# Reordered loads, transposes and fill in the opening batches of an attention kernel fused with a feed-forward

## The chip, the cores and the metric

The kernel runs on one core of one Trainium2 chip. The metric is the device time of one execution in microseconds; less is better. Three runs of the kernel before gave 258.54, 258.21 and 256.69 us, a median of 258.21.

## What is computed

Two steps in a row. The attention first: for each of 8 batches and 8 heads, 32 "packed" query rows `p` attend over 576 keys and values of width 64, and the 576 rows of `q` then attend over the 32 packed results. The feed-forward follows on the 4608 rows of width 512 (8 heads x 64) that come out.

```python
p_packed = sm_attn(p, k, v)                 # softmax(p k^T / 8) v      [8, 8, 32, 64]
out = sm_attn(q, p_packed, p_packed)        #                           [8, 8, 576, 64]
x = out.transpose(0, 2, 1, 3).reshape(4608, 512)
h = x @ w_in                                # w_in  [512, 2048]
g = h * cos(h)
result = g @ w_out                          # w_out [2048, 512], fp32 out
```

## The kernel before

The eight batches pass one after another through the same steps, and the kernel writes the order of every instruction by hand (there is no scheduler: each engine runs its instructions in the order in which the source emits them, and waits where an operand is missing). Matmuls are in bf16. PSUM has eight banks: two belong to the output tiles (`ot`), six are handed out either as three pairs (`psA`) or as six single banks (`psH`); `banks(3)` and `banks(0)` change between the two.

The steps of one batch `b`:

- `load(n, b)`: a DMA that GpSimd issues brings k, q or v to SBUF and casts it to bf16. The v and q buffers are single: the next load waits until the last one has been read. All such DMAs go through GpSimd's queue in order, and reuse eight semaphores in turn, so that the ninth waits for the first to land.
- `pe_T`: k and q are transposed on TensorE in three groups of eight 96x96 blocks, each group copied out of PSUM by the engine named (later batches use the transposing DMA, `xbar`). `permute_v` rearranges v, on VectorE for batch 0 and on GpSimd after that.
- `dup_p`, `pack_p`: the packed rows p are cast, doubled, transposed and kept in `P2`.
- `s1`: scores of p against k, and the exponential on ScalarE (tile `a`, its sums beside it). `a1_pe` or `a1_one` transposes these probabilities on TensorE into `a1T`; `recips` takes reciprocals of the sums; `pp` multiplies by v and copies the result into `ppT`.
- `s2`: scores of q against `ppT`, the exponential (`a2u`); `sums2` takes the sums by a matmul and their logarithm; `normalise` turns these into the reciprocal on ScalarE and writes the weights `a2n` on VectorE.
- `ppw(b, n)`: `ppT` times quarter n of `w_in`, copied to `PPW`. With it, h is `PPW` times `a2n` and never needs the attention's output itself.
- the h steps: for each of 16 slices `fc` of the 2048 columns, matmuls into PSUM, the cosine on ScalarE (`cosT`) and the product on VectorE (`gT`). Batch 0 uses `h_one` (512 of 576 columns, one `psH` bank each; the other 64 columns come later in `h_rest`), the others `h_mm`, inside `slot`.
- the output: `gT` times `w_out`, 16 matmuls of 128x512 for each 128 rows, one bank `ot`. These matmuls are the fill: `fill(n)` emits the next n of them between other work, `set_filler(b)` starts the generator of batch b, and `fill(1000)` emits all that is left. `slot` spreads what is left over its 16 h steps.

Batch 0 has no earlier batch to fill with. There `warm(n)` emits n matmuls on zeros, whose result is not used. The opening is straight-line code, lines 385 to 464, then `slot(1, ...)`, the opening of batch 2 at lines 505 to 533, and a regular loop from line 537. In the opening, `a1_one(1)` at line 436 transposes the probabilities of batch 1 into the two halves of one `psA` pair; after it come `banks(0)` and the 16 `h_one` steps, with the packed blocks `ppw(0, 1..3)` after steps 1, 5 and 9 and `pp(1)` after step 13:

```python
    a1_one(1)
    recips(1)
    banks(0)
    for fc in range(NFC):
        h_one(0, fc)
        if fc in (1, 5, 9):
            ppw(0, 1 + fc // 4, (ACT, V), own=True)
        if fc == 13:
            pp(1, own=True, engs=(ACT, ACT))
    ACT.preload_act_table_set(EXP_SET)
    pe_T("q", 1, (ACT, V, V), own=one)
```

## Time and profile before

| what | value |
|---|---|
| profiled execution, its own time | 258.04 us |
| its span | 256.3 us |
| median of three runs (range) | 258.21 us (256.69 to 258.54) |
| TensorE busy, matmuls | 235.0 us, 92% |
| VectorE busy | 161.4 us, 63% |
| ScalarE busy | 174.3 us, 68% |
| GpSimd busy | 56.3 us, 22% |
| DMA moved | 37.09 MB, mean 145 GB/s |
| q-load of batch 0 lands, first q transposes | 14.02 us |
| first `h_one` matmul of batch 0 | 24.29 us |
| `s2` of batch 1 begins | 40.19 us |
| second half of the first `h_mm` of batch 1 begins | 48.75 us |

In the views, PE is TensorE's matmuls, PEld its weight loads, DVE is VectorE, ACT ScalarE, POOL GpSimd, SP the engine that issues output DMAs. A row of a timeline is start, duration, engine, source line, operation, output tile, input tile, shapes, and how many instructions are merged; in brackets, how long the engine stood idle before it and what released it. The chain of waits is the path that ended last, followed back from the end: start, duration, what. Line 86 is the copy helper on VectorE, line 84 on ScalarE.

### The profile page before, as it was taken

Reading aid. Unit: us, or ns where it says so; the run is one execution under the profiler, and the core shown is the slowest. Engines: PE = TensorE matmul, PEld = TensorE weight load, DVE = VectorE, ACT = ScalarE, POOL = GpSimd, SP = SyncE. Lnnn points to the kernel's source line nnn. Section 1 sums busy time; section 2 is a strip of 40 time slices with the busy share of each in tenths; the row PEclk is TensorE's granted clock in tenths of the full one; section 3 lists DMA queues with packets and bytes.
Section 4 is the critical chain, followed back from the end, with each engine's and each line's share of the span. In section 5 each row is a group of like instructions: output and inputs, shape, how many; then the busy total and the mean of one; then the engine's idle time right before and its main releaser. Section 6 shows DMA issues by size and latency. Waiting matters only on the chain.

```text
span 256.3 us, 5021 instructions
## 1 busy us (share of the span) xinstructions
PE 235.0 (92%) x2000; PEld 130.0 (51%) x2035; DVE 161.4 (63%) x239; ACT 174.3 (68%) x293; POOL 56.3 (22%) x67
## 2 busy tenths in 40 slices
PE   8684876899998999999999999999999999999993
PEld 3452242366553565456545654465546554665452
DVE  3456984677656778757875667568857765675000
ACT  2366897576736888788888767788788675975110
POOL 8253611340070040504050303103310000000000
PEclk9999797999999999999999999999999999999999
DMA  7999999999679999499969993999692111202133
GB/s 102 202 206 205 205 207 224 204 151 185 135 131 202 215 169 224 96 192 166 196 141 196 167 221 77 154 199 139 141 169 71 41 43 41 75 18 62 52 84 82
DMA packets 63159, 37.09 MB, mean 145 GB/s; under 512 B 35776, under 2 KB 58560, under 8 KB 63136
## 3 DMA queue, kind: packets, MB, share of 16 engines
q0 software_dynamic: 23152, 18.75, 48.2%
q1 hardware_dynamic: 39824, 17.90, 33.5%
q8 instruction: 16, 0.26, 0.4%
q10 hardware_dynamic: 160, 0.13, 0.2%
q14 instruction: 7, 0.06, 0.1%
HBM read 37.22 MB, written 9.44 MB: 182 GB/s over the span
## 4 chain that ended last, share of the span: by engine, by line
PE 76%; DVE 9%; ACT 6%; DMA 4%; issue 3%; POOL 1%; DVEq 0%; ACTq 0%; POOLq 0%
PE ot L346 43%; PE psA L261 21%; DMA qbf<-in_q_dram 4%; DVE gT L291 2%; DVE PPW L86 2%; PE psA L141 2%; PE psA L214 2%; PE psA L240 2%; DVE gT L268 1%; PE psA L190 1%; PE ot L332 1%; DVE a2n L250 1%; ACT cosT L265 1%; PE psH L287 1%; ACT a2u L232 1%
## 5 line engine op out<-in xcount | busy, mean ns | idle before, releaser
L346 PE MATMUL ot<-w_out_bf,gT 128*128 128x512 bf16 x482 | 128.4, 383 | 2.0 <-issue 0.9
L268 DVE TENSOR_TENSOR gT<-psA,cosT 128x576 bf16<-128x576 f32 x112 | 83.3, 757 | 34.5 <-ACT cosT L265 33.5
L265 ACT ACTIVATE cosT<-psA 128x576 bf16<-128x576 f32 x112 | 72.5, 652 | 26.2 <-PE psA L261 24.6
L261 PE MATMUL psA<-a2n,PPW 128*128 128x288 bf16 x448 | 73.4, 286 | 1.2 <-DVE PPW L86 0.4
L346 PEld LDWEIGHTS <-gT 128*128 128x128 bf16 x512 | 47.9, 98 | 43.3 <-issue 7.0
L261 PEld LDWEIGHTS <-PPW 128*128 128x128 bf16 x448 | 43.7, 98 | 31.2 <-issue 2.0
L86 DVE CAST PPW<-psA 128x1024 bf16<-128x1024 f32 (+1 forms) x23 | 25.8, 1129 | 12.1 <-PE psA L214 12.0
L272 POOL COPY joint<-gT 128x512 bf16<-128x512 bf16 x14 | 8.6, 611 | 104.4 <-DVE gT L268 104.4
L86 DVE COPY osb<-ot 128x512 f32<-128x512 f32 (+1 forms) x14 | 9.4, 672 | 21.3 <-PE ot L332 17.4
L84 ACT COPY osb<-ot 128x512 f32<-128x512 f32 (+1 forms) x23 | 13.2, 574 | 13.5 <-PE ot L346 12.4
L86 POOL COPY vp<-vbf 96x3072 bf16<-96x3072 bf16 x7 | 19.3, 2750 | 3.5 <-DMA vbf<-in_v_dram 3.5
L250 DVE SCALAR_TENSOR_TENSOR a2n<-a2u,r,lns 128x576 bf16<-128x576 bf16 x16 | 12.7, 833 | 5.8 <-ACT lns L248 5.8
L242 ACT ACTIVATE lns<-psA 128x576 f32<-128x576 f32 x16 | 10.4, 650 | 7.3 <-PE psA L240 6.7
L150 ACT ACTIVATE a<-psA 128x576 bf16<-128x576 f32 x16 | 10.2, 646 | 4.2 <-PE psA L141 4.2
L84 ACT CAST ppT<-psA 64x128 bf16<-64x128 f32 x24 | 6.2, 259 | 9.2 <-DVE ppT L86 5.6
L346 PE MATMUL ot<-w_out_bf,joint 128*128 128x512 bf16 x47 | 12.4, 380 | 0.0
L232 ACT ACTIVATE a2u<-psA,rs 128x576 bf16<-128x576 f32 x16 | 11.0, 736 | 1.8 <-PE psA L214 0.8
L291 DVE TENSOR_TENSOR gT<-psH,cosT 128x512 bf16<-128x512 f32 x16 | 10.2, 685 | 2.5 <-ACT cosT L290 2.4
L290 ACT ACTIVATE cosT<-psH 128x512 bf16<-128x512 f32 x16 | 8.9, 604 | 3.8 <-PE psH L287 3.4
L287 PE MATMUL psH<-a2n,PPW 128*128 128x512 bf16 x30 | 9.2, 426 | 2.1 <-DVE PPW L86 1.2
L214 PE MATMUL psA<-w_in_bf,ppT 64*32 64x512 bf16 x224 | 10.4, 381 | 0.5 <-DVE gT L268 0.5
L248 ACT ACTIVATE lns<-lns 128x576 f32<-128x576 f32 x16 | 10.0, 674 | 0.0
(80 smaller groups left out, 178.1 us busy)
## 6 DMA issues: line engine op xcount, KB each, us to landing
kbf<-in_k_dram POOLq DMA_DIRECT2D x8, 576.0 KB, 12.3
vbf<-in_v_dram POOLq DMA_DIRECT2D x8, 576.0 KB, 8.0
qbf<-in_q_dram POOLq DMA_DIRECT2D x8, 576.0 KB, 9.8
out_dram<-osb SPq DMA_DIRECT2D x24, 192.0 KB, 2.9
out_dram<-osb SPq DMA_DIRECT2D x22, 128.0 KB, 2.4
w_in_bf<-in_moe_w_in_dram POOLq DMA_DIRECT2D x4, 512.0 KB, 16.7
w_out_bf<-in_moe_w_out_dram POOLq DMA_DIRECT2D x4, 512.0 KB, 20.7
out_dram<-osb SPq DMA_DIRECT2D x26, 64.0 KB, 2.2
```

The costliest lines, as they stand in the source:

```text
L84: ACT.copy(out=out, in_=in_)
L86: eng.tensor_copy(out=out, in_=in_)
L214: nc.tensor.matmul(ps[y][32 * x:32 * x + 32, :], ppT[b % 2][r, 2 * x + y, :], w_in_bf[r, x, n * 512:(n + 1) * 512], start=True, stop=True)
L232: ACT.activation(out=a2u[b][:, y].rearrange("p (e x) -> p e x", e=2), in_=ps[y][:, :, 0:HS], func=AF.Exp, scale=rs1[b][:, y:y + 1])
L242: ACT.activation(out=lns[b][:, y].rearrange("p (e x) -> p e x", e=2), in_=ps[:, :, 0:HS], func=AF.Ln)
L250: V.scalar_tensor_tensor(out=a2n[b][:, y], in0=a2u[b][:, y], scalar=r1[b][:, y:y + 1], in1=lns[b][:, y], op0=ALU.mult, op1=ALU.mult)
L261: nc.tensor.matmul(ps[:, e, 0:HS], PPW[b][:, y, fc * 128:(fc + 1) * 128], a2n[b][:, y, e * HS:(e + 1) * HS], start=(y == 0), stop=(y == 1))
L265: ACT.activation(out=csv, in_=ps[:, :, 0:HS], func=AF.Sin, bias=PI_HALF)
L268: V.tensor_tensor(out=gT[b][:, fc, :].rearrange("p (e x) -> p e x", e=2), in0=ps[:, :, 0:HS], in1=csv, op=ALU.mult)
L287: nc.tensor.matmul(ps, PPW[b][:, y, fc * 128:(fc + 1) * 128], a2n[b][:, y, 0:512], start=(y == 0), stop=(y == 1))
L291: V.tensor_tensor(out=gT[b][:, fc, 0:512], in0=ps, in1=cs, op=ALU.mult)
L346: nc.tensor.matmul(pss[c], w, w_out_bf[:, fc, :], start=(fc == 0), stop=(fc == NFC - 1))
```

## The change

- At the start the load of p by SP takes only batch 0's rows; batch 1's come by a separate load on GpSimd's queue after k of batch 1, and are cast by VectorE (`dup_p(2, 4, V)`) after `s2(0)` and packed (`pack_p(1, 2, ...)`) after the k transposes of batch 1, in place of one of two `warm` matmuls.
- The last quarter of `w_in` is loaded before v of batch 1, not after it.
- The probabilities of batch 1 are transposed by `a1_pe` into two single `psH` banks; `a1_one` goes.
- `ppw(0, 1..3)` come after h steps 0, 4 and 8; `pp(1)` after the last h step; q of batch 1 is copied out by VectorE alone, and the load of the exponential's table on ScalarE comes after that in the source.
- Of the fill before `slot(1, ...)` (4, 4 and 6 around `ppw(1, 1)` and `normalise(1)`), the four ahead of `ppw(1, 1)` go to the end (4 and 10).
- In batch 2's opening, `fill(6)` after `pp(2)` becomes `fill(8)`, and `fill(4)` moves from behind `recips(3)` to ahead of `s1(3)`.

```diff
-    def a1_pe(b, ys=(0, 1)):
+    def a1_pe(b, ys=(0, 1), own=None):
...
-            ps = psa(BF16)[:, 0, :]
+            ps = own(BF16) if own else psa(BF16)[:, 0, :]
...
-    def a1_one(b):
-        t = a1T[b] = att_pool.tile([128, 2, C, 128], BF16, name="a1T", tag="a1T")
-        ps = psa(BF16)
-        for y in range(2):
-            for c in range(C):
-                nc.tensor.transpose(ps[0:TP, y, c * 128:(c + 1) * 128], a1[b % 2][:, y, c, 0:TP], ident)
-            copy(V, t[0:TP, y].rearrange("p c x -> p (c x)"), ps[0:TP, y, 0:C * 128])
...
-    nc.sync.dma_start(out=p_raw[:, 0:4, :], in_=p_rows[:, 0:4, :])
+    nc.sync.dma_start(out=p_raw[:, 0:2, :], in_=p_rows[:, 0:2, :])
...
     load("k", 1)
+    G.dma_start(out=p_raw[:, 2:4, :], in_=p_rows[:, 2:4, :])
...
-    dup_p(0, 4, V)
-    pack_p(0, 2)
+    dup_p(0, 2, V)
+    pack_p(0, 1)
...
-    load("v", 1)
     load_w_in(3)
+    load("v", 1)
...
     s2(0)
+    dup_p(2, 4, V)
...
-    warm(2)
+    pack_p(1, 2, bank(BF16))
+    warm(1)
...
-    a1_one(1)
-    recips(1)
     banks(0)
+    a1_pe(1, own=one)
+    recips(1)
     for fc in range(NFC):
         h_one(0, fc)
-        if fc in (1, 5, 9):
+        if fc in (0, 4, 8):
             ppw(0, 1 + fc // 4, (ACT, V), own=True)
-        if fc == 13:
-            pp(1, own=True, engs=(ACT, ACT))
+    pp(1, own=True, engs=(ACT, ACT))
+    pe_T("q", 1, (V, V, V), own=one)
     ACT.preload_act_table_set(EXP_SET)
-    pe_T("q", 1, (ACT, V, V), own=one)
...
     sums2(1, 1)
-    fill(4)
     ppw(1, 1, V)
     fill(4)
     normalise(1)
     ACT.preload_act_table_set(SIN_SET)
-    fill(6)
+    fill(10)
...
     pp(2)
-    fill(6)
+    fill(8)
...
     normalise(2)
+    fill(4)
     s1(3)
     ACT.preload_act_table_set(SIN_SET)
     a1_xbar(3)
     recips(3)
-    fill(4)
```

More of the change, by code (lines that the diff above doesn't have):

```diff
@@ L408 @@
     permute_v(0, V)
+    load_w_in(3)
     load("v", 1)
-    load_w_in(3)
     warm(3)
@@ L435 @@
     rest_ppw()
-    a1_one(1)
+    banks(0)
+    a1_pe(1, own=one)
     recips(1)
-    banks(0)
     for fc in range(NFC):
         h_one(0, fc)
-        if fc in (1, 5, 9):
+        if fc in (0, 4, 8):
             ppw(0, 1 + fc // 4, (ACT, V), own=True)
-        if fc == 13:
-            pp(1, own=True, engs=(ACT, ACT))
+    pp(1, own=True, engs=(ACT, ACT))
+    pe_T("q", 1, (V, V, V), own=one)
     ACT.preload_act_table_set(EXP_SET)
-    pe_T("q", 1, (ACT, V, V), own=one)
     load("v", 2)
```

## The prediction

> **What bounds the kernel now.** The page first: where TensorE idles, and where its clock drops.

> ```profile
> PE   8684876899998999999999999999999999999993
> ...
> PEclk9999797999999999999999999999999999999999
> ```

> One digit is 6.4 us. From slice 8 (51 us) TensorE is at nine tenths to the end: there a microsecond is gained only by taking away a gap or a matmul. Before it come the 4, 8, 7, 6 of slices 3 to 6, with a 7 in the clock of slices 4 and 6. All but two small edits of the change lie in this opening. So next the chain of waits, 19 to 49 us:

> ```profile
> 22.64 0.47 DVE a1T L86
> 23.11 0.04 issue
> 23.15 0.51 PE psA L182 x6
> 23.66 0.02 issue
> 23.68 0.56 DVE a1T L86
> 24.25 0.04 issue
> 24.29 1.40 PE psH L287 x4
> ...
> 39.34 0.81 ACT qT L84
> 40.15 0.04 issue
> 40.19 0.44 PE psA L141 x16
> ...
> 43.59 1.71 PE ot L346 x4
> ...
> 45.72 1.23 DVE PPW L86
> ```

> Three places. At 22.64 the two halves of the probabilities go through one PSUM pair in turn: copy, transposes, copy, and only then the first h matmul (24.29). At 39.34 the scores of batch 1 wait for a q copy on ScalarE. At 43.59 four fill matmuls stand ahead of `ppw(1, 1)`, whose copy (45.72) `a2n` queues behind. The timeline of VectorE, between the first two:

> ```profile
> 31.14 2.48 DVE L291 TENSOR_TENSOR gT<-psH,cosT 128x512 bf16<-128x512 f32 x4
> 33.54 0.68 DVE L86 CAST PPW<-ot 128x512 bf16<-128x512 f32 x1
> 34.13 2.49 DVE L291 TENSOR_TENSOR gT<-psH,cosT 128x512 bf16<-128x512 f32 x4
> 37.57 1.29 DVE L291 TENSOR_TENSOR gT<-psH,cosT 128x512 bf16<-128x512 f32 x2 [0.95 <-ACT cosT L290]
> ```

> A product takes 0.60 (31.14 to 33.54 for four), a `PPW` copy 0.60. VectorE is the bound of the h steps, with 16 + 3 such pieces, 11.4 us; they took from 25.59 to 38.86, 13.27. ScalarE needs 16 x 0.56 + 3 x 0.53 = 10.6, warm TensorE 16 x 0.52 + 3 x 0.41 = 9.6.

> **The change part by part**, in times of this execution (258.04 us, 0.17 under the median).

> *Single banks.* The second half's transposes no longer wait for the first half's copy. Both halves still wait for the second exponential of `s1(1)`, 21.35 (the new tiles lie where its scores were); 12 transposes by 0.08 end at 22.5, behind VectorE's `PPW` copies (22.64). The first h matmuls follow at once, ready 0.67 later as before (24.29 to 24.96), at 23.2; ScalarE's table is in at 22.86, the cosine done at 23.8. VectorE runs two `a1T` copies (22.64 to 23.6), reciprocals (0.35), and starts products at 24.0, not 25.59: 1.6 gained.

> *Packed blocks a step sooner, `pp(1)` last.* A block's copy now has three products between it and the first step that needs it (1.8 us) where it had two (1.2), against a matmul and a cosine of 0.67 + 0.60; that should remove the short idles (0.24 and 0.16). ScalarE's four `ppT` copies (35.84, 1.08 us) move behind the last cosine and with them the 0.95 idle of VectorE. Products end at 24.0 + 11.4 + 0.3 for small gaps = 35.7, against 38.86.

> *q copies on VectorE alone.* Three copies, two of which took 1.01 together: 1.5, so `s2(1)` starts at 37.2 where it started at 40.19. ScalarE's table load (1.28) hides: `ppT` copies until 35.4, table until 36.7. **3.0 gained** up to here. The old path (table, then a 0.80 copy) would be no quicker: were the cover gone, 0.8 + 0.04 comes back.

> *Quarter before v1, p in two loads.* The queue of loads runs without a gap, about 2.9 us for a k, q or v and 2.6 for a quarter of weights: quarter 0 lands at 19.5, 1 at 22.1, 2 at 24.65, v1 at 27.5, quarter 3 at 30.2. 384 KB of p at the end took 2.7 us, so the new 64 KB cost 0.45, and everything behind moves by this. Quarter 3 then lands at 27.7, before its use at about 28.7 (after step 8); v1 at 30.5. GpSimd's copy of v1 (2.75) ends at 33.3, where it ended at 31.3; behind it in GpSimd's queue stand only loads that queue in the DMA anyway. `pp(1)` has its turn when step 15 is through, about 33.5, and must be 2.7 ahead of `s2(1)`: slack 1.2. If that cover is gone, each microsecond costs one. w_out's first chunk lands at 36.1, before the first fill at 37.8. The smaller first load frees SP nothing that the chain uses: it starts with k and q at the DMA's rate. Zero.

> *New on VectorE after `s2(0)`*: two casts, first waiting for the new p load, with the three k copies and `a2n` queued behind. It lands 0.45 after k1 (16.9): 17.35; the casts of twice the size took 0.59 for both, so 0.3; the first k copy starts at 17.65, not 17.45, and the pause before the second (0.21) takes it up. The new `P2` copy (half of a 0.42) ends at 19.7, `a2n` starts at 19.77. `s1(1)` comes 0.4 later, but ScalarE is busy until 20.20. Lowest price 0. The highest comes from line 160:

> ```profile
> 75.74 1.66 DVE L160 TENSOR_SCALAR rs<-r 128x2 f32<-128x2 f32 x1
> ```

> Its other instances take 0.17; GpSimd's copy `vp` ran from 74.61 to 77.37, when this one ended. The new casts meet GpSimd's DMA issues (0.77 each, two of them around 17.2 to 18.7); held until the end they start 1.35 late and cost 1.2. I take 0, because the casts at 3.10 ran beside GpSimd's work at 3.21 without it. [...]

> *Fill(4) behind `ppw(1, 1)`.* VectorE's copy comes up to 1.7 sooner (1.71 of fill). But the 14 fill matmuls and the block stand before the h matmuls either way, and TensorE was full from 43.59 to 47.9; the second half of the first h matmul came at 48.75. At half clock (0.43 a matmul until 45.3) they end at 48.0, not 48.75: **0.7**. At full clock the two fill matmuls between the sums take 0.43, not 0.85, which also removes ScalarE's idle of 0.68 at 43.62; the block is through at 43.3, its copy at 44.6, `a2n` 1.7 later at 46.3, and the 14 matmuls (0.216 each, 3.0) end with it: 2.4. Which one it is hangs on the clock:

> ```profile
> 21.30:24.70 3.40, 1.13 (x12) 0.76 (x11) 2.59 (x9) 1.55 (x3) 0.74 (x1) 1.00 1.27 204
> 24.70:28.20 3.50, 3.28 (x15) 0.95 (x15) 2.30 (x4) 2.46 (x5) 1.46 (x2) 0.51 1.28 209
> 38.40:41.85 3.45, 1.10 (x27) 0.65 (x29) 2.27 (x4) 2.65 (x4) 1.11 (x2) 1.00 1.24 229
> 41.85:45.30 3.45, 3.45 (x18) 1.22 (x16) 0.35 (x1) 2.77 (x5) 0.00 (x0) 0.51 1.23 219
> ```

> Columns: window, length, then busy time of PE, PEld, DVE, ACT, POOL, then clock. Twice a window with TensorE busy for a third (1.13, 1.10) is followed by one at half clock; the window from 17.9 with 2.35 was not. The first falls away (TensorE idles only 20.6 to 21.4); the second gap shrinks from 2.5 us to 1.7, so the window holds some 1.4 of work: nearer to 1.10 than to 2.35, so I take the half clock. [...]

> *Batch 2.* `fill(8)`: TensorE idled 0.35 before the scores of 78.91, which wait for ScalarE's `ppT`; two more matmuls (0.43) fill it and are taken from slot 2: 0.35. `fill(4)` ahead of `s1(3)`: its second half idled 0.38 for ScalarE's logarithm; that is filled, but the cosine of 86.13 stays where the table load puts it, and I count 0.25. From neither to both: 0 to 0.75.

> Sum: 3.0 + 0.7 + 0.35 + 0.25 = 4.3 of 258.04: **253.7 us**. Bounds: 1.2 less for the casts, 1.7 more for the clock.

> **The rivals.** (1) No half-clock window around 42 us: 258.04 - 6.0 = 252.0. For it: the gap shrinks; against: 1.4 is nearer to 1.10. (2) v1 lands behind q1 as well (33.4) and `pp(1)` becomes the bound: copy until 36.2, `s2(1)` at 38.9, 1.7 lost: 255.4. Against it: the loads land in the order of issue. (3) The h steps do not run at VectorE's pace; only the 1.6 of the banks stays: 256.4. For it: the old steps lost 1.9 to idles, ScalarE's 10.6 is close. (4) Slower: the new wait of VectorE for p. Its price is landing minus 17.55, and it is paid by k copies, `a2n` and all behind. With quarter 0 (19.95) it leaves a gain of 1.9; from 21.9 on it decides the sign; with quarter 2 (25.1) the time is 261.3. Against it: order of landing; for it: its rows are 256 bytes and were never seen between large loads.

> **How the numbers follow.** Forecast 0.40; (1) 0.27; (2) 0.12; (3) 0.11; (4) and anything slower 0.10. The range reaches from 251.5 (rival 1 without the 0.3 of gaps, batch 2's edits at their 0.75) to 257.0 (rival 3 with half the casts' 1.2); outside stays (4). This kernel's measurement tells 1%, 2.6 us, from no change. Below 255.6 lie forecast, (1) and a third of (2): 0.71; above 260.8 lies most of (4): 0.08; the rest 0.21.

> **What would show it.** First `gT` of line 283 near 24.0 and `s2` of batch 1 near 37.2; VectorE without idle between; the k copies of batch 1 still from 17.5; clock 1.0 from 24 to 28; first `h_mm` complete about 3.7 sooner than 48.75; the lead kept to the end. Wrong if VectorE idles at its `p_bf` cast, if `pp(1)` waits for `vp`, or if the lead at 50 us is lost by 100.

## The result, and the profile after

| | before | after |
|---|---|---|
| median of 20 runs each (range), us | 258.19 (255.71 to 258.86) | 256.80 (252.81 to 259.05) |
| ratio, with its 95% interval | | 0.9892 [0.9859, 0.9924] |
| profiled execution: time, span, us | 258.04, 256.3 | 255.21, 253.3 |

The changed kernel is 0.5 to 1% faster: the forecast of 253.7 was too low by 3.1, and the median lies 0.2 inside the upper end of the range. The ratio leaves out runs more than 1.5% above the fastest of the same kernel, which are ten of after's 20, while the medians of all 20 stand as 0.9946. What is new beside the level is the scatter: 6.2 us, where before had 3.2.

From the page of the kernel after, TensorE's share and granted clock in 40 slices of 6.3 us:

```profile
PE   8788869999999699999999999999999999999993
...
PEclk9999979999999979999999999999999999999999
```

The 4, 8, 7, 6 of slices 3 to 6 have become 8, 8, 6, 9, and of the clock's two dips there (slices 4 and 6) one is left, in slice 5. But there is a 6 in slice 13 (82 to 89 us) and a 7 in the clock of slice 14, where before has nines. The chain of waits of the kernel after (start, duration, what) shows both ends:

```profile
21.97 0.93 DVE a1T L86 x2
22.90 0.08 DVE r L159
22.98 0.02 issue
23.01 0.17 DVE rs L160
23.18 0.59 DVE gT L283
23.77 0.60 DVE PPW L86
24.36 2.39 DVE gT L283 x4
...
34.53 1.40 DVE qT L86 x3
35.93 0.04 issue
35.97 0.68 PE psA L141 x16
...
83.67 0.52 PE psA L253 x4
84.20 4.68 DMA a1T<-a
88.88 0.14 issue
89.01 0.86 PE psA L182 x24
```

From 20.84 to 35.93 the chain is VectorE alone, without a pause: the copies of both halves together, products from 23.18, the q copies at 34.53, `s2(1)` at 35.97. That is the opening as forecast. At 84.20 stands something that before's chain did not have: 4.68 us of the transposing DMA of batch 3's probabilities (`a1_xbar(3)`, issued by SP), for which `pp(3)` waits in slot 2. TensorE's timeline after, around it (idle before, and releaser, in brackets):

```profile
86.12 0.65 PE L253 MATMUL psA<-a2n,PPW 128*128 128x288 bf16 x4
89.01 0.86 PE L182 MATMUL psA<-a1T,vp 96*128 96x64 bf16 x24 [2.23 <-DMA a1T<-a]
90.22 1.17 PE L253 MATMUL psA<-a2n,PPW 128*128 128x288 bf16 x4
```

2.23 us idle, and then matmuls at 1.8 times their duration (1.17 for 0.65). In the timeline of before the same `pp(3)` ran at 93.42 without idle.

The lead of after over before, by time in the two profiled executions, then reads so: first k copies 0.67 (8.71 to 8.04); first product 2.5; `s2(1)` 4.2; first full-width product of batch 1 5.8 (49.88 to 44.10); `s2(2)` 6.0; `pp(3)`, if it had not waited, 6.6 (93.42 to about 86.8); `pp(3)` as it ran 4.4; `s2(3)` 2.9 (104.4 to 101.5); end 3.0. So the opening and batch 2 brought 6.6, and 3.6 were given back between 86 and 93 us: 2.2 of waiting and about 1.5 of half clock.

Why did the transfer come late? The issues of SP (start, duration of the issue, what) in the kernel before:

```profile
58.97 4.72 SPq L102 DMA_TRANSPOSE qT<-qbf  x1
...
79.86 3.66 SPq L102 DMA_TRANSPOSE qT<-qbf  x1
83.61 3.11 SPq L102 DMA_TRANSPOSE kT<-kbf  x1
86.82 1.52 SPq L164 DMA_TRANSPOSE a1T<-a  x1
```

and in the kernel after:

```profile
55.37 6.98 SPq L102 DMA_TRANSPOSE qT<-qbf  x1
...
75.84 3.74 SPq L102 DMA_TRANSPOSE qT<-qbf  x1
79.67 3.16 SPq L102 DMA_TRANSPOSE kT<-kbf  x1
82.92 1.18 SPq L344 DMA_DIRECT2D out_dram<-osb  x2
84.20 2.38 SPq L164 DMA_TRANSPOSE a1T<-a  x1
```

Before, the last line was issued at 86.82 and landed some 4.1 later, near 90.9, when `pp(3)` was wanted at 93.42: it had 2.5 us to spare. After, it is wanted 6.6 sooner but issued only 2.6 sooner. About 1.3 of what is missing are the two output stores at 82.92: the `fill(4)` that now stands ahead of `s1(3)` puts them in front of the transfer, where before, and e4 below, have them behind it. Also ahead of it in SP's queue stand the transposes of q and k of the next batches, and these wait for loads. Those loads stand behind the `gate` copy on GpSimd, which waits until k of batch 3 is transposed, and that copy ran at 72.55 before and at 68.82 after: 3.7 sooner, while `s2(2)` was 6.0 sooner. The compute moved forward and the transfers, which are paced by each other, moved less.

### The profile page after: what moved, and what is told of

The parts are those of the page before. It is cut to its first block, busy times and chain, and to the rows that moved or that the text cites. A ratio compares the mean times of both kernels' runs of the same rounds, so it can differ in the third digit from the quotient of the medians.

```text
span 253.3 us, 5058 instructions
## 1 busy us (share of the span) xinstructions
PE 237.5 (94%) x2034; PEld 130.2 (51%) x2034; DVE 159.6 (63%) x243; ACT 173.4 (68%) x292; POOL 57.0 (23%) x68
## 4 chain that ended last, share of the span: by engine, by line
PE 77%; DVE 8%; ACT 3%; DMA 2%; issue 0%; DVEq 0%
PE ot L338 46%; PE psA L253 20%; DVE gT L283 4%; PE psA L206 3%; PE psA L141 2%; DMA a1T<-a 2%; PE psA L182 2%; PE psA L232 1%; DVE gT L260 1%; PE ot L324 1%; DVE PPW L86 1%; ACT cosT L257 1%; ACT a L150 1%; DVE qT L86 1%; ACT L519 1%; DVE joint L296 0%
## 5 line engine op out<-in xcount | busy, mean ns | idle before, releaser
L338 PE MATMUL ot<-w_out_bf,gT 128*128 128x512 bf16 x512 | 134.1, 383 | 0.0
L260 DVE TENSOR_TENSOR gT<-psA,cosT 128x576 bf16<-128x576 f32 x112 | 83.1, 756 | 38.7 <-ACT cosT L257 37.8
L253 PE MATMUL psA<-a2n,PPW 128*128 128x288 bf16 x448 | 74.2, 289 | 0.3 <-DVE gT L260 0.3
L253 PEld LDWEIGHTS <-PPW 128*128 128x128 bf16 x448 | 44.2, 99 | 31.3 <-issue 2.1
L86 DVE CAST PPW<-psA 128x1024 bf16<-128x1024 f32 (+1 forms) x23 | 25.8, 1128 | 10.5 <-PE psA L206 10.5
L86 DVE COPY osb<-ot 128x512 f32<-128x512 f32 (+1 forms) x14 | 9.4, 672 | 21.3 <-PE ot L324 17.4
L84 ACT COPY osb<-ot 128x512 f32<-128x512 f32 (+1 forms) x23 | 13.2, 575 | 13.5 <-PE ot L338 12.4
L86 POOL COPY vp<-vbf 96x3072 bf16<-96x3072 bf16 x7 | 19.2, 2749 | 5.0 <-DMA vbf<-in_v_dram 5.0
L84 ACT CAST ppT<-psA 64x128 bf16<-64x128 f32 x24 | 6.2, 260 | 10.8 <-DVE ppT L86 4.8
L279 PE MATMUL psH<-a2n,PPW 128*128 128x512 bf16 x32 | 8.1, 381 | 1.3 <-DVE PPW L86 1.3
```

What stands on the lines that cost most here:

```text
L84: ACT.copy(out=out, in_=in_)
L86: eng.tensor_copy(out=out, in_=in_)
L253: nc.tensor.matmul(ps[:, e, 0:HS], PPW[b][:, y, fc * 128:(fc + 1) * 128], a2n[b][:, y, e * HS:(e + 1) * HS], start=(y == 0), stop=(y == 1))
L260: V.tensor_tensor(out=gT[b][:, fc, :].rearrange("p (e x) -> p e x", e=2), in0=ps[:, :, 0:HS], in1=csv, op=ALU.mult)
L338: nc.tensor.matmul(pss[c], w, w_out_bf[:, fc, :], start=(fc == 0), stop=(fc == NFC - 1))
```

## The experiments

Two theories stood against each other: that the lead was lost to the new wait of `pp(3)`, and that it was never worth more (TensorE full from 51 us in any case). Runs e1 to e4 start from the kernel after; f1 to f4, f6 and f7 start from e1, in which the late wait is gone; f5 starts from before. Medians are of 4 to 12 runs each, and ratios are to the kernel before on the same chip. Runs e1 to e4, f1 to f4 and f5 to f7 were made on three chips, on which the kernel before had medians of 258.32, 258.19 and 258.07.

### e1: batch 3's probabilities transposed on TensorE

```diff
-    a1_xbar(3)
     recips(3)
...
-    fill(9)
+    fill(5)
+    a1_pe(3)
+    fill(4)
```

> Edit on the kernel after: the probabilities of batch 3 are transposed on TensorE (a1_pe(3), 12 transposes and two VectorE copies between fill(5) and fill(4)), not by the transposing DMA. Theory A (the lead of 6.8 us that the kernel after has at 86 us falls to 3.0 because pp(3) waits 2.23 us for this DMA and the clock then drops for a window, 1.4 us): no wait ahead of pp(3), no half-clock window at 90 to 93 us; 3.6 less 0.7 for the added transposes, so a span near 250.4 and a time near 252.3 beside 255.2. Theory B (the DMA as a whole has become the bound, and the next load is waited for in its place): pp(3) does not wait, but another wait of 2 to 4 us follows by 120 us, time 254.5 to 256.

Measured: 251.50 (251.29 to 256.00), ratio 0.9748 [0.9706, 0.9789], 2.5% faster than before; profiled execution 251.29, span 249.5. TensorE's timeline in e1:

```profile
36.00 0.44 PE L141 MATMUL psA<-qT,ppT 64*32 64x288 bf16 x16 [0.90 <-DVE qT L86]
...
86.81 0.86 PE L182 MATMUL psA<-a1T,vp 96*128 96x64 bf16 x24
```

`s2(1)` starts where it started in after (35.97), and `pp(3)` runs at 86.81 with no idle before it: the wait was what the lead was lost to. The sum closes. From after's span of 253.3 go the wait (2.2), the half clock behind it (1.5), and another half-clock window at 36 us that this execution did not have (1.0: first full-width product at 43.09, not 44.10); 12 transposes on TensorE come on top (0.08 each, 1.0). That gives 249.6, against 249.5 measured. With the wait gone, five of six runs fell within 1 us of each other. e1 is the best version of the study.

### e2: the same transfer earlier in SP's queue

```diff
     xbar("q", 3)
-    xbar("k", 4)
...
     a1_xbar(3)
+    xbar("k", 4)
```

> Edit on the kernel after: the transposing DMA of batch 3's probabilities is issued on SP ahead of the one of batch 4's k, not behind it; nothing else. Theory A (place in SP's queue): it lands near 84 us, before pp(3) wants it at 86.8; the 2.23 us wait and the half-clock window go, span near 249.7, time near 251.6. Theory B (DMA as a whole): k of batch 4 and with it the loads that wait for it come 1 to 2 us later, and a wait of that size shows in batch 4; time 253.5 to 255.5. Theory C (the wait is for the softmax of batch 3 itself, not for the queue): the transposing DMA starts no earlier than 84 us, time as after, 255 to 256.

Measured: 252.87 (251.57 to 253.94), ratio 0.9795 [0.9750, 0.9840]. SP's issues in e2:

```profile
74.89 3.98 SPq L102 DMA_TRANSPOSE qT<-qbf  x1
...
81.63 1.51 SPq L164 DMA_TRANSPOSE a1T<-a  x1
83.23 4.23 SPq L102 DMA_TRANSPOSE kT<-kbf  x1
```

Issued at 81.63, not 84.20, the transfer costs no wait: `pp(3)` ran at 88.13 without idle. So it is its place behind k's transpose, not the transfer itself, that made it late. e2 spares TensorE the 12 transposes and is still 1.4 above e1. Its profiled execution had a half-clock window at 35 to 39 us, which e1's did not have, and TensorE idled 1.08 us before `s2(2)`. The idle comes from VectorE and GpSimd:

```profile
69.82 2.89 DVE L160 TENSOR_SCALAR rs<-r 128x2 f32<-128x2 f32 x1
69.92 2.76 POOL L86 COPY vp<-vbf 96x3072 bf16<-96x3072 bf16 x1
```

A scaling of 128x2 numbers, 0.17 us in e1, lasted until GpSimd's copy of v ended, and the `ppT` copy that `s2(2)` needs stands behind it on VectorE. From `pp(2)` to the first packed block behind `s2(2)` e2 took 4.38 us (70.26 to 74.64), e1 2.78: 1.6 lost. With 0.87 lost up to `pp(2)` and the 1.0 of the transposes saved, that gives 1.5 over e1, against spans of 250.8 and 249.5. Both losses come before 75 us, where the first instruction that the edit moves would have run, so they are scatter and not the edit's.

### e3: p in one load again

```diff
-    nc.sync.dma_start(out=p_raw[:, 0:2, :], in_=p_rows[:, 0:2, :])
+    nc.sync.dma_start(out=p_raw[:, 0:4, :], in_=p_rows[:, 0:4, :])
...
-    G.dma_start(out=p_raw[:, 2:4, :], in_=p_rows[:, 2:4, :])
...
-    dup_p(0, 2, V)
-    pack_p(0, 1)
+    dup_p(0, 4, V)
+    pack_p(0, 2)
...
-    dup_p(2, 4, V)
...
-    pack_p(1, 2, bank(BF16))
-    warm(1)
+    warm(2)
```

> Edit on the kernel after: p of batches 0 and 1 comes again in one load of 128 KB by SP at the start, both are packed there, and the warm matmul is back. Theory A (the smaller first load lets the first k land sooner): the first k transposes start at 8.16 us as before, not at 7.49, and the scores of q of batch 1 start 0.67 later than 35.97 at 36.6; time 0 to 0.7 above the kernel after. Rival (scatter of one execution, or the loads of k run beside p): first k transposes at 7.5 us, scores at 35.9. In either case VectorE has no p_bf cast at 16.4 and the k copies of batch 1 are not earlier by more than 0.1.

Measured: 256.07 (254.10 to 257.90), ratio 0.9916 [0.9881, 0.9950], not to be told from after's 0.9892. In the profiled execution the first k copies came at 8.76 (after: 8.04) and `s2(1)` at 36.7 (35.97), as if the split were worth 0.7; but `pp(3)` waited 4.4 us there, so on this base the total says nothing of the opening. f6 repeats it on e1.

### e4 and f1: the fill where it was

```diff
     sums2(1, 1)
+    fill(4)
     ppw(1, 1, V)
...
-    fill(10)
+    fill(6)
...
     pp(2)
-    fill(8)
+    fill(6)
...
-    fill(4)
     s1(3)
...
     recips(3)
+    fill(4)
```

The same four edits, in e4 on the kernel after and in f1 on e1.

> Edit on the kernel after: the four fill edits are undone (4, 4, 6 ahead of slot 1; 6 after pp(2); fill(4) behind recips(3)). Theory (they are worth 1 us or more on the path of the opening, more where the clock is full): the first h matmuls of batch 1 complete 0.7 to 2.2 us later than 43.4, TensorE idles 0.3 to 0.8 between 70 and 78 us; at 86 us the lead over the kernel before is 6.8 less 1.5 to 2.8. As pp(3) waits for a DMA in any case, the end is 0 to 1.5 us later. Rival (fill is conserved work and its place is worth nothing): first h matmuls of batch 1 within 0.3 us of 43.4, lead unchanged.

> Base: the kernel after with batch 3's probabilities transposed on TensorE (251.5 us; the wait of pp(3) that hid every gain of the opening is gone there). Edit: the four fill edits undone. Theory (sizes from the first two profiles with a full clock, where the first h matmuls of batch 1 end 5.7 us after the scores with the new fills and 6.3 with the old): 0.6 there and 0.4 to 0.7 in batch 2, so 1.0 to 1.3 later, 252.5 to 252.8. Prediction's own sizes: 0.7 or 2.4 there and 0.6 in batch 2, 252.8 or 254.5. Rival (fill is conserved): within 0.3 of 251.5.

Measured: e4 254.93 (253.79 to 255.72), ratio 0.9875 [0.9825, 0.9924]; f1 251.65 (251.45 to 255.15), ratio 0.9797 [0.9748, 0.9846]. e4 is no slower than after: `pp(3)` waited there too (2.67) and ran at 89.07, where after has 89.01, so that an edit ahead of the wait does not show behind it. f1, without the wait, shows the local effects, a first full-width product at 43.60 against 43.09 in e1 and 0.39 of idle before `s1(3)`, and the total is 0.15 above e1 (spans 249.9 and 249.5). The fill edits are worth about 0.4, less than the runs scatter: a miss for the 1.0 and more that was expected of them.

### f2: the probabilities of batch 1 in one pair again

```diff
-    banks(0)
-    a1_pe(1, own=one)
+    a1_one(1)
     recips(1)
+    banks(0)
```

with `a1_one` as it stood in before.

> Same base. Edit: the probabilities of batch 1 go through one psA pair again, before banks(0). Theory: the products of batch 0 start 1.6 to 1.75 us later (24.8 in place of 23.1) and nothing takes it up, because VectorE runs without a gap from there: time 253.1 to 253.3, more if the clock then drops for a window (TensorE idles about 2.5 us more). Rival (the pause only moves: v of batch 1 and its copy on GpSimd set the start of pp(1), for which TensorE waited 1.2 us): less than 0.5 later.

Measured: 256.10 (255.38 to 257.03), ratio 0.9927 [0.9902, 0.9952], 4.6 above e1. VectorE's timeline in f2:

```profile
22.07 0.55 DVE L86 COPY a1T<-psA 96x768 bf16<-96x768 bf16 x1
23.20 0.55 DVE L86 COPY a1T<-psA 96x768 bf16<-96x768 bf16 x1 [0.59 <-PE psA L182]
...
25.11 0.69 DVE L291 TENSOR_TENSOR gT<-psH,cosT 128x512 bf16<-128x512 f32 x1 [1.08 <-ACT cosT L290]
...
26.59 0.69 DVE L291 TENSOR_TENSOR gT<-psH,cosT 128x512 bf16<-128x512 f32 x1 [0.19 <-ACT cosT L290]
```

The two idles (0.59 between the copies, 1.08 before the first product) put the products at 25.11, where e1 has 23.05: 2.06. Of this 0.22 stood there before the pair (`a2n` at 19.28 and at 19.06), so the pair's own price is 1.84, close to the 1.6 to 1.75 expected. The idles of 0.16 to 0.19 after it come with the half clock from 24.3 to 27.7 us (e1: full), behind 3.41 us in which TensorE was busy for only 1.13; they make 2.8 at `s2(1)`. Another 1.5 is lost at `pp(2)`, where GpSimd's copy of v held line 160 as in e2 (2.78 at 71.65). In the profiled execution 2.06, 0.75 and 1.5 add up to 4.3, against spans of 253.7 and 249.5. So the total of 4.6 is not the edit's own wait alone.

### f3: the h loop as before

```diff
-        if fc in (0, 4, 8):
+        if fc in (1, 5, 9):
             ppw(0, 1 + fc // 4, (ACT, V), own=True)
-    pp(1, own=True, engs=(ACT, ACT))
-    pe_T("q", 1, (V, V, V), own=one)
+        if fc == 13:
+            pp(1, own=True, engs=(ACT, ACT))
     ACT.preload_act_table_set(EXP_SET)
+    pe_T("q", 1, (ACT, V, V), own=one)
```

> Same base. Edit: the loop of h steps as in the kernel before (blocks after steps 1, 5, 9; pp(1) after 13; the table load before the q copies and one of them on ScalarE). Theory: VectorE idles some 0.4 at the blocks and 0.95 at pp(1), and the scores wait for ScalarE's q copy: 1.4 to 1.9 later, 252.9 to 253.4; as v of batch 1 lands later than in the kernel before, pp(1) after step 13 also waits for its copy, up to 1 us more. Rival (TensorE's matmuls set the pace of the h steps): less than 0.5.

Measured: 255.63 (255.37 to 256.76), ratio 0.9926 [0.9901, 0.9951], 4.1 above e1. VectorE's timeline in f3:

```profile
18.04 0.36 DVE L370 CAST p_bf<-p_raw 128x128 bf16<-128x128 f32 x2 [2.48 <-DMA p_raw<-in_p_dram]
...
36.98 1.29 DVE L283 TENSOR_TENSOR gT<-psH,cosT 128x512 bf16<-128x512 f32 x2 [0.96 <-ACT cosT L282]
```

The 0.96 idle behind `pp(1)`'s copies on ScalarE is back, and TensorE waited 2.5 for ScalarE's q copy: both as in before. The first line is something else: here the late part of p landed 1.7 us later than in after (cast at 18.04 against 16.38), though nothing ahead of it was edited, and the weights `a2n` came 1.07 later than in e1. The half clock from 19.4 to 26.2 us followed, and the first product came at 25.53, 2.48 behind e1 (23.05), before anything that the edit moves. From there to `s2(1)` (39.6, 3.6 behind e1) another 1.1 is lost; this is the loop's own part, less than the 1.4 to 1.9 expected. Behind TensorE's wait of 2.5 the clock was half from 39.8 to 43.3, which costs 1.3 more, and line 160 was held at `pp(2)` (1.76), 0.5. The profiled execution is the longest of ten (256.76). All ten lie within 1.4 us, but what the shorter ones lost, and how often p is late in them, is not known.

### f4: v1 loaded before the last quarter again

```diff
-    load_w_in(3)
     load("v", 1)
+    load_w_in(3)
```

> Same base. Edit: v of batch 1 is loaded ahead of the last quarter of w_in again. Theory: the quarter lands near 29.9 us, TensorE reaches the block that needs it at 27.7 and stands 2.2 us; VectorE has three products in hand, so the products end 0.5 to 1.0 later and the time is 252.0 to 252.5; pp(1) no longer waits for vp. Rival (what gains is v1's wait going): 251.0 to 251.3.

Measured: 255.24 (254.75 to 256.91), ratio 0.9911 [0.9881, 0.9940], 3.7 above e1. One line of TensorE's timeline in f4:

```profile
30.19 0.63 PE L206 MATMUL ot<-w_in_bf,ppT 64*32 64x512 bf16 x8 [2.46 <-DMA w_in_bf<-in_moe_w_in_dram]
```

and of VectorE's:

```profile
30.91 0.69 DVE L86 CAST PPW<-ot 128x512 bf16<-128x512 f32 x1 [1.24 <-PE ot L206]
32.45 0.69 DVE L283 TENSOR_TENSOR gT<-psH,cosT 128x512 bf16<-128x512 f32 x1 [0.85 <-ACT cosT L282]
33.30 0.69 DVE L283 TENSOR_TENSOR gT<-psH,cosT 128x512 bf16<-128x512 f32 x1 [0.16 <-ACT cosT L282]
```

The last packed block waits 2.46 for its weights, VectorE loses 1.24 and 0.85, and then 0.16 at each of five products, because TensorE runs at half clock (0.50 from 29.2 to 36.1 us) and ScalarE's cosines wait for it. Nearly all of it is in the opening: `s2(1)` at 39.45, 3.45 behind e1; the held line 160 (1.77) adds 0.5 at `pp(2)`. A miss: 0.5 to 1.0 had been expected. With steps that run 4 us sooner, the quarter's place is no detail but a condition.

### f5: only e1's step, on the kernel before

```diff
-    a1_xbar(3)
     recips(3)
...
-    fill(9)
+    fill(5)
+    a1_pe(3)
+    fill(4)
```

> Edit on the kernel before: batch 3's probabilities are transposed on TensorE, as in the run that brought the kernel after to 251.5. Theory (the wait of pp(3) is new, made by the change: in the kernel before a1T(3) landed at 90.9 us and pp(3) wanted it at 93.4): no gain, 0 to 0.7 us slower for the 12 added transposes, 258.2 to 258.9. Rival (the transposing DMA of batch 3 costs any kernel, by what it does to the queue of SP or to the other transfers): 1 us or more faster, 257 or less.

Measured: 259.19 (256.61 to 259.76, and one run of 354.02 with a mean clock of 0.655), ratio 1.0043 [1.0016, 1.0070]. On before the step gains nothing and costs about 1.1, more than the 0 to 0.7 expected and close to the 1.0 of its 12 transposes: there was no wait of `pp(3)` to remove. The wait belongs to the change.

### f6: p in one load, on e1

The diff is that of e3.

> Base: the kernel after with batch 3's probabilities transposed on TensorE (251.5 us). Edit: p of batches 0 and 1 in one load of 128 KB by SP at the start again. Theory (the first k lands 0.7 later and nothing takes it up, while the loads behind come 0.3 to 0.45 sooner): first k copy at 8.7 us, not 8.0, scores of q of batch 1 at 36.7, time 252.0 to 252.4. Rival (the split is worth nothing, because a stretch set by transfers follows): 251.3 to 251.7.

Measured: 251.76 (251.32 to 254.86), ratio 0.9810 [0.9760, 0.9861], 0.26 above e1, with `s2(1)` at 36.2 (e1: 36.0). In the total the split is worth nothing that can be measured. The 0.67 by which after's first k copies were ahead is not all scatter: with p whole they came at 8.71, 8.76, 8.75 and 8.26 in four kernels, split between 7.97 and 8.27 in nine; f6 has the 8.26, so its execution shows little of that lead.

### f7: the late part of p on ScalarE's queue, on e1

```diff
-    G.dma_start(out=p_raw[:, 2:4, :], in_=p_rows[:, 2:4, :])
...
     s1(0)
+    ACT.dma_start(out=p_raw[:, 2:4, :], in_=p_rows[:, 2:4, :])
```

> Same base. Edit: batch 1's rows of p are loaded by ScalarE's DMA queue after s1(0), not by GpSimd's after k of batch 1. Theory (in one of ten profiles VectorE stood 2.48 us for this load, which then landed near 18.0 and not 16.3; a queue of its own takes that away, and the other loads come some 0.3 sooner): VectorE's p_bf cast waits for nothing beyond 15.9 us, time 251.0 to 251.5, no run above 254. Rival (the load competes with k and q wherever it is issued): k copies of batch 1 no earlier, 251.5 or more.

Measured: 255.73 (251.91 to 256.17), ratio 0.9854 [0.9797, 0.9911]. Two lines of VectorE's timeline in f7:

```profile
16.23 0.36 DVE L370 CAST p_bf<-p_raw 128x128 bf16<-128x128 f32 x2 [0.56 <-DMA p_raw<-in_p_dram]
17.23 1.74 DVE L86 COPY kT<-ot 128x768 bf16<-128x768 bf16 x3 [0.64 <-PE ot L116]
```

The casts came 0.15 sooner than in after, but the k copies behind them 0.44 later (16.79 there). The clock was half from 21.4 to 24.8 us and from 38.4 to 41.9; `s2(1)` started at 37.2, and line 160 was held by GpSimd's copy (3.26 at 71.78), which cost 2.0 of the 4.8 us between the spans (254.3 and 249.5). No gain, and a theory that fell: the casts still waited for p, until 16.23, and the k copies came no sooner. What the edit itself costs is not separated from the clock and the hold. The one run as short as e1's had a mean clock of 0.998, the other five 0.983 to 0.987.

## Why the prediction came out as it did

*Single banks: right.* Forecast 1.6 at the first product. After has 2.5, of which 0.67 were there from the first k copies on: 1.8. f2 puts the pair's price at 1.84.

*h loop at VectorE's pace: right.* From first product to last, 13.27 before and 11.45 after (23.08 to 34.53), forecast 11.7; no idle of VectorE in it. f3 brings the old idle back.

*q copies on VectorE: right.* From there to `s2(1)` 1.44, forecast 1.5.

*Quarter before v1: right in place, and more than it was credited with.* GpSimd's copy of v1 ended at 33.0 (forecast 33.3); `pp(1)` waited 0.97 for it, but `s2(1)` was released by VectorE's q copies, so the slack of 1.2 was there. The prediction priced what the swap could cost; f4 shows that without it 3.45 of the opening are lost.

*p in two loads, the new casts: zero, as forecast.* f6 gives 0.26, not to be told from zero. The two casts took 0.36 at 16.38 while GpSimd issued two loads from 16.47 on, and again 0.36 at 16.23 in f7, where the issue had begun first (16.14), so the hold of 1.2 on VectorE did not come. GpSimd's copy of v, which the prediction took its highest price from, does hold line 160 (1.66 to 3.26 us in place of 0.17), in seven of the 13 profiled executions. The fourth rival's mechanism, p landing late with all of VectorE behind it, is real: in f3 the weights came 1.07 late by it. It did not decide the sign.

*Fill behind `ppw(1, 1)`: the term was mis-sized, through the clock.* Forecast 0.7 at half clock or 2.4 at full; from `s2(1)` to the first full-width product after is 1.6 quicker than before (8.13 against 9.69), and e1, at full clock, 2.6 (7.09). By f1 against e1, both at full clock there, the fill gives 0.44 of it (7.53 against 7.09). The rest is the half-clock window, which came as forecast but lay elsewhere: 41.85 to 45.3 before, where it cost 2.2 (9.69 against 7.53), 35.4 to 38.9 after, where it costs 1.0 (8.13 against 7.09). That it came at all is luck: TensorE's busy time ahead of it was 1.95 of 3.41 us and not the 1.4 that was reckoned, and e1, with the same code up to here, kept the full clock.

*Batch 2: one gap right, one put down to the wrong cause.* Both gaps (0.35 and 0.38) are gone in after, and the lead grows from 6.0 to 6.6; in the total it is not seen. The 0.38 is `fill(4)`'s: with the old fill it is back in f1 (0.39). The 0.35 was not a want of fill. In before line 160 was held until GpSimd's copy ended, the 1.66 of the row that the prediction shows, and `ppT` was late by it; in f1, with `fill(6)` and an unheld line 160 (0.17), TensorE does not idle there.

*The signs.* All three that were to mean "wrong" showed, and only one of them cost anything. VectorE idled 0.79 at its `p_bf` cast in after, but had stood 1.20 at the same place before; `pp(1)` waited 0.97 for `vp`, within its slack; the lead was lost by 100 us.

*The step that failed* is "from slice 8 (51 us) TensorE is at nine tenths to the end", read as "the lead is kept". A busy TensorE was taken to mean that nothing else had a due time. The transposing DMA of batch 3's probabilities had 2.5 us of slack in before; a gain of 6.6 ahead of it uses that up and turns the excess into a wait. It was not among the rivals, though the text named the sign by which it would show (the lead at 50 us gone by 100). So it is luck that the 4.3 of the forecast and the 2.8 of the profiled execution (1.4 between the medians) are no further apart: two errors have opposite signs, as the part ahead of 86 us gave 6.6 and not 4.3, and 3.6 were given back. e1 (wait gone, faster), e2 (earlier in the queue, wait gone) and f5 (no wait in before, no gain) show the cause.

The scatter has, in part, the same root, as far as three executions show. In the profiled executions of kernels with the late transfer the wait was 2.2, 2.7 and 4.4 us, and the one with 4.4 was the longest of them (257.79); without the wait most runs of e1 and f1 agree within 1 us. The single longer runs of e1 (256.00), f1 (255.15) and f6 (254.25 and 254.86) were not profiled; their mean clock was 0.985 to 0.993, where the runs up to 251.8 us of these kernels have 0.996 to 1.000. Of the six kernels made from e1, those whose profiles show half-clock windows (f2, f3, f4, f7; mean clock 0.980 to 0.992) have medians of 255.2 to 256.1, the others (f1, f6; 0.997 and 1.000) 251.7 and 251.8. The same four also had line 160 held, which e1, f1 and f6 had not; by the profiles it accounts for 0.5 to 2.0 of their 3.8 to 5.4 us over e1. How often each of the two falls in the runs that were not profiled stays open.

## What to carry to other kernels

Before an opening is made shorter, list the transfers that later steps wait for, each with landing time and wanted time: the smallest slack, not the share of the busiest engine, says how much of the gain is kept. If it is too small, move that transfer ahead in its queue, or take it off the queue, together with the change. And judge the parts of a change on a base whose later wait is removed: e4 was hidden by the wait and f1 was not.

## What the runs showed of the hardware that was not expected

A pause of TensorE in the opening can cost more than its length. f2's 2.06 became 2.8 at `s2(1)`, f4's 2.46 became 3.45: the clock granted was half for 3.41 us after the one and for 6.83 after the other, and where TensorE then sets the pace, everything behind is late.

```profile
32.03:35.44 3.41, 1.95 (x49) 1.84 (x49) 3.41 (x8) 2.79 (x8) 1.94 (x3) 1.00 1.24 206
35.44:38.85 3.41, 2.88 (x30) 1.18 (x30) 1.71 (x3) 2.58 (x4) 1.33 (x2) 0.50 1.24 207
86.64:90.05 3.41, 1.18 (x28) 0.93 (x27) 1.45 (x2) 0.79 (x2) 2.63 (x5) 1.00 1.03 187
90.05:93.46 3.41, 3.41 (x14) 1.70 (x12) 0.76 (x1) 2.20 (x6) 0.32 (x1) 0.50 1.14 155
```

and of e1, where the code up to here is the same, counted from the moment of its first full clock (6.76 us):

```profile
30.66:34.07 3.41, 2.25 (x35) 1.29 (x34) 3.41 (x7) 2.39 (x4) 3.11 (x2) 1.00 1.26 206
34.07:37.48 3.41, 2.38 (x53) 1.56 (x50) 2.63 (x5) 3.27 (x7) 1.69 (x3) 1.00 1.24 206
```

The windows of e1 lie 1.37 us ahead of those of after, so the same pauses of TensorE are shared out differently between them: 1.95 us of work were followed by half clock, 2.25 and 2.38 were not. Counted so over all 13 executions, up to 245 us, each of the ten windows with less than 1.65 us of work at full clock was followed by half clock, none of the 870 with 2.06 or more, and four of the nine between 1.88 and 2.05. Between two half-clock stretches the full clock, too, held for whole numbers of that length: 13.66 us in before (28.11 to 41.77, four windows) and 51.20 in after (38.85 to 90.05, fifteen). And a window need not be idle for the half clock to follow: 1.18 us of work in 3.41 (86.64 to 90.05) were followed by a clock of 0.50.

A large copy on GpSimd can hold a tiny instruction on VectorE for as long as it runs. Line 160 took 1.66 to 3.26 us and not 0.17 in seven of the 13 profiled executions (before, e2, f2, f3, f4, f5, f7), each time until GpSimd's copy of v (2.76) ended; in the six others the two did not meet. After, e1 and e2 have the same code up to there, and the copy began at 70.89, 73.95 and 69.92: whether the two meet changes from execution to execution.

The issue of a transposing DMA of q or k took SP 3.0 us (q at 132.11 in before) to 8.2 us (q at 55.71 in e1; 7.0 at 55.37 in after), and what stood behind it in that queue was held up: in after q was issued at 75.84, k at 79.67, the two stores at 82.92 and the probabilities at 84.20. And a small load did not land at a fixed place among large ones: the same 64 KB of p were there for a cast at 16.38 in after and at 18.04 in f3.
